# A decode attention kernel: the value stream two tiles behind the key stream, the last values in finer pieces, loops on DVE and ACT as on TensorE

## The chip, the cores and the metric

The kernel runs on one core of a Trainium2 chip. The metric is the device time of one execution in microseconds (us); lower is better. The kernel before took 664.19 us (median of 3 runs, 663.47 to 664.40). The profile gives a span, from the first to the last instruction, which is about 2 us shorter than the device time. Engines are named as the profile names them: PE is TensorE (PEld its weight loads), DVE the vector engine, ACT the scalar engine, POOL is GpSimd, and SP issues the loads. SBUF is the on-chip memory, PSUM the one that takes TensorE's products. The releaser of a wait is what ended it.

## The reference

One token per sequence (4 sequences) attends to a cache of 8192 positions with 8 key/value heads of width 256; each pair of query heads shares one. The result is projected with `wo` and multiplied by a gate from a small MLP-like block.

```python
def _A_ref(x, k_cache, v_cache, wq, wo):                 # x: 4 x 1 x 448
    q = (x @ wq).reshape(B, 1, 16, 256).transpose(0, 2, 1, 3)
    k = jnp.repeat(k_cache, 2, axis=1)                   # cache: 4 x 8 x 8192 x 256, bf16
    v = jnp.repeat(v_cache, 2, axis=1)
    p = softmax(einsum("bhqd,bhkd->bhqk", q, k) * 256 ** -0.5)
    o = einsum("bhqk,bhkd->bhqd", p, v)
    return o.transpose(0, 2, 1, 3).reshape(B, 1, 4096) @ wo
xn = layernorm(A_x)
out = A_x + _A_ref(xn, ...) * silu(_B_ref(xn, ...))      # B: two layernorms, gelu, small weights
```

What matters: 32 tiles (4 sequences x 8 heads), each with 4 MiB of keys and 4 MiB of values, which are read once. With the weights that is 279 MB.

## The kernel before

Keys and values have two slots each in SBUF. For each tile `h` TensorE transposes the keys in 16 groups (`f_t`), DVE and ACT copy the transposed groups out of PSUM, and TensorE forms the scores (`f_s`). Maximum, exponentials and row sum follow. The products of tile `h - 1` with its values (`f_pv`, 128 of them) are spread through the end of tile `h`. TensorE runs this in a hardware loop over pairs of tiles; DVE, ACT and GpSimd have all 32 tiles written out. SP issues all loads on one queue, so the order of its program is the order of the stream.

```python
    PV_PARTS = (0, 12, 24, 44, 72, 100, NPV)
    NPIECE = 4
    ...
            def load_k(h):
                if h >= 2:
                    sp.wait_ge(S["p_t"], NGR * (h - 1))          # keys of h-2 transposed
                sp.dma_start(kn_dst(h), A_k_cache[b, g]...)
            def load_v(h):
                if h == 0:  sp.wait_ge(S["p_h2"], 1)
                else:       sp.wait_ge(S["p_pv"], h)             # products of h-2 done
                ...                                              # the last one in 4 equal pieces
            load_k(0); load_k(1); <wo>; load_v(0)
            for h in range(2, NH):
                load_k(h)
                load_v(h - 1)
            load_v(NH - 1)
    ...
            def body(h):                                         # TensorE, inside its loop
                for j in range(NGR):
                    f_t(h, j)
                    if j >= LAG: f_s(h, j - LAG)
                tail = [three last f_s] + [f_rmaxT(h), f_bc(h), f_sum(h)]
                for i, f in enumerate(tail):
                    f_pv(h - 1, PV_PARTS[i], PV_PARTS[i + 1])
                    f()
    ...
            for h in range(NH):                                  # DVE, written out 32 times
                for j in D_GROUPS: evac(v, h, j)
                f_rmax(h); f_diag(h); f_negb(h); f_ot(h - 1); f_rz(h)
    ...
            take("v_ot")                                         # TensorE, behind its loop
            for g in range(HKV - 1): f_o(g)                      # 7 of 8 output groups, 16 products each
            for i in range(NPIECE):  <last value products, 32 for each piece>
            take("v_ot"); f_o(HKV - 1)
```

## Time and profile before

| | kernel before |
|---|---|
| device time | 664.19 us |
| span of the profiled run | 661.7 us |
| bytes read | 278.99 MB, 98.4% of the DMA engines' span |
| TensorE / DVE / ACT busy | 82% / 39% / 39% |
| last keys landed / last value byte landed | 635.47 / 655.04 us |
| last value product ended | 658.16 us |

The head of the page of the kernel before, with the DMA lines: share of the span per engine, then per fortieth of the span the busy tenths and the GB/s, then the queues (packets, MB, share of 16 engines).

```profile
span 661.7 us, 27809 instructions
PE 543.4 (82%) x12935; PEld 535.1 (81%) x12935; DVE 256.4 (39%) x577; ACT 255.3 (39%) x358; POOL 9.3 (1%) x44
DMA  8999999999999999999999999999999999999993
GB/s 362 436 408 432 422 434 432 428 436 432 430 434 428 436 430 428 438 430 430 436 426 434 434 424 440 428 432 434 428 432 436 424 438 432 430 434 430 428 420 156
...
q1 hardware_dynamic: 12288, 278.99, 98.4%
q8 instruction: 11, 0.18, 0.1%
q14 instruction: 8, 0.07, 0.0%
...
```

The stream is full from the second fortieth to the last but one, so this kernel lives at the speed of its DMA. Queues q8 and q14 carry the engines' own programs.

The next lines are from the timeline of the kernel before, for its end (start, duration, engine, line, operation, count, and in brackets the idle time before and what ended it).

```profile
635.57 3.35 PE L469 MATMUL pst<-ident_b,kn 128*128 128x128 bf16 x32 [2.16 <-PEq L421]
...
652.08 2.72 PE L537 MATMUL pst<-wo_sb,OT 128*4 128x112 bf16 x112 [0.18 <-PEq L421]
654.73 0.61 PE L550 MATMUL psv<-pT,vb 128*128 128x32 bf16 x16
...
657.61 0.55 PE L550 MATMUL psc<-pT,vb 128*128 128x32 bf16 x16
658.21 0.17 DVE L396 TENSOR_TENSOR OT<-psv,rz 128x2 bf16<-128x2 f32 x1 [6.10 <-PE psc L550]
...
658.58 0.37 PE L537 MATMUL pst<-wo_sb,OT 128*4 128x112 bf16 x16 [0.42 <-PEq L421]
...
659.62 0.69 SPq L159 DMA_DIRECT2D out_dram<-out_b  x2
```

The last keys land at 635.47 and TensorE begins at 635.57. From there it has no idle time worth naming until the last value product ends at 657.61 + 0.55 = 658.16: 22.7 us of work from the last key. The finish is 3.54 us. The last value byte had landed 3.1 us before that product ended, so at this end TensorE is late, not the stream.

The trace also records each landing on the semaphores, 16 counts for each load. The Trainium skill (DMA: Bandwidth & Descriptors, section "Why a DMA increments its semaphore by 16 and not by 1") says why: a load runs on up to 16 engines that finish independently, and each posts its own count. The trace agrees: the counts of a load are spread. First and last landing of some loads, in us (load 6 is `wo`; from there on keys and values alternate, in another order after the change):

```
load number        6       10      21      41      61      67 (V30)   71 (last piece)
before, first    47.87    86.79  193.61  387.87  582.13   640.41     650.34
before, last     49.73    90.04  196.89  391.19  585.93   645.19     655.04
```

From load 21 to load 67 the first engine takes 9.713 us for each load of 4 MiB. The distance between first and last grows from 1.9 to 4.8 us. The load is done only with the last one. "First engine" and "last engine" below mean the first and the last landing of a load, as the records name no engine.

### The profile page before, as it was taken

How to read it: one execution, taken by the hardware profiler on the slowest of the kernel's cores; microseconds unless marked ns; L12 is line 12 of the kernel's file. 1: busy time of each engine (PE TensorE's matmuls, PEld its weight loads, DVE VectorE, ACT ScalarE, POOL GpSimd, SP SyncE). 2: the span in 40 equal slices, each digit the busy share in tenths (PEclk: the TensorE clock that was granted, in tenths of full speed). 3: DMA queues.
4: the chain of work that ended last, by engine and by line, in shares of the span. 5: the costliest groups of instructions: out<-in, count | busy, mean ns of one | idle time of the engine just before them, and what ended most of it. 6: DMA issues, size and time to landing. Idle time of an engine off the chain costs nothing. (4 is left out here: it accounts for less than half of the span.)

```text
span 661.7 us, 27809 instructions
## 1 busy us (share of the span) xinstructions
PE 543.4 (82%) x12935; PEld 535.1 (81%) x12935; DVE 256.4 (39%) x577; ACT 255.3 (39%) x358; POOL 9.3 (1%) x44
## 2 busy tenths in 40 slices
PE   2387798889878878988888898878898888789787
PEld 2387797789878878988788898878898788789787
DVE  6233253334433334433334443333344333344332
ACT  1044253344443334444333444433344433344441
POOL 2000000000000000000000000000000000000000
PEclk9988698898877889878789987878988778898788
DMA  8999999999999999999999999999999999999993
GB/s 362 436 408 432 422 434 432 428 436 432 430 434 428 436 430 428 438 430 430 436 426 434 434 424 440 428 432 434 428 432 436 424 438 432 430 434 430 428 420 156
DMA packets 12331, 279.24 MB, mean 422 GB/s; under 512 B 1172, under 2 KB 3224, under 8 KB 3480
## 3 DMA queue, kind: packets, MB, share of 16 engines
q1 hardware_dynamic: 12288, 278.99, 98.4%
q8 instruction: 11, 0.18, 0.1%
q14 instruction: 8, 0.07, 0.0%
q10 hardware_dynamic: 24, 0.01, 0.0%
HBM read 278.99 MB, written 0.00 MB: 422 GB/s over the span
## 5 line engine op out<-in xcount | busy, mean ns | idle before, releaser
L469 PE MATMUL pst<-ident_b,kn 128*128 128x128 bf16 x4096 | 354.4, 244 | 80.7 <-PEq L421 80.7
L469 PEld LDWEIGHTS pst<-ident_b,kn 128*128 128x128 bf16 x4096 | 287.9, 111 | 82.5 <-issue 82.5
L239 ACT ACTIVATE kT<-pst 128x1024 bf16<-128x1024 bf16 x224 | 229.3, 1024 | 231.9 <-PE pst L469 231.9
L237 DVE COPY kT<-pst 128x1024 bf16<-128x1024 bf16 x288 | 197.8, 692 | 268.3 <-PE pst L469 268.3
L481 PE MATMUL psc<-qc,kT 128*128 128x2 bf16 x4096 | 176.8, 164 | 1.0 <-issue 1.0
L481 PEld LDWEIGHTS psc<-qc,kT 128*128 128x128 bf16 x4096 | 157.4, 98 | 1.1 <-issue 1.1
L507 PE MATMUL psv<-pT,vb 128*128 128x32 bf16 x4096 | 131.8, 177 | 5.7 <-issue 3.1
L507 PEld LDWEIGHTS psv<-pT,vb 128*128 128x128 bf16 x4096 | 117.8, 97 | 6.8 <-issue 5.9
L260 ACT ACTIVATE pT<-psc,negb 128x64 bf16<-128x64 f32 x64 | 20.2, 332 | 144.5 <-DVE negb L384 144.5
L372 DVE TENSOR_REDUCE rmax<-psc 128x2 f32<-128x128 f32 x32 | 9.3, 292 | 42.1 <-PE psc L481 42.1
L396 DVE TENSOR_TENSOR OT<-psv,rz 128x2 bf16<-128x2 f32 x65 | 7.6, 162 | 30.1 <-PE psv L507 24.0
L498 PE MATMUL psm<-rowsum,ones_f 128*128 128x2 f32 x64 | 11.8, 253 | 8.5 <-PEq L421 8.5
L498 PEld LDWEIGHTS psm<-rowsum,ones_f 128*128 128x128 f32 x64 | 9.9, 195 | 10.8 <-issue 10.8
L377 DVE TENSOR_REDUCE gmax<-psm 2x1 f32<-2x128 f32 x32 | 8.9, 279 | 17.6 <-PE psm L489 17.6
L493 PE MATMUL psm<-diag,ones_f 2*128 2x2 f32 x64 | 11.6, 248 | 4.5 <-PEq L421 3.9
L493 PEld LDWEIGHTS psm<-diag,ones_f 2*128 2x128 f32 x64 | 9.8, 190 | 6.8 <-issue 4.0
L230 POOL COPY qc<-qT 128x4 bf16<-128x4 bf16 x32 | 6.0, 188 | 599.9 <-PE psc L481 587.1
L384 DVE COPY negb<-psm 128x2 f32<-128x2 f32 x32 | 5.1, 160 | 21.4 <-PE psm L493 21.4
L260 ACT ACTIVATION_READ_ACCUMULATOR pT<-psc,negb 128x1 f32 x64 | 12.6, 196 | 0.0
L427 PE MATMUL pst<-ident_b,xn_b 4*128 4x4 bf16 x14 | 0.6, 161 | 12.6 <-DVE xn_b L306 8.0
L427 PEld LDWEIGHTS pst<-ident_b,xn_b 4*128 4x128 bf16 x14 | 0.5, 99 | 12.7 <-issue 7.9
L388 DVE RECIPROCAL rz<-psm 128x2 f32<-128x2 f32 x32 | 5.5, 171 | 12.6 <-PE psm L498 12.6
(68 smaller groups left out, 70.7 us busy)
## 6 DMA issues: line engine op xcount, KB each, us to landing
kn<-in_A_k_cache_dram SPq DMA_DIRECT2D x32, 4096.0 KB, 27.2
vb<-in_A_v_cache_dram SPq DMA_DIRECT2D x31, 4096.0 KB, 32.3
vb<-in_A_v_cache_dram SPq DMA_DIRECT2D x4, 1024.0 KB, 17.9
vb<-in_A_wq_dram SPq DMA_DIRECT2D x1, 3584.0 KB, 11.5
wo_sb<-in_A_wo_dram SPq DMA_DIRECT2D x1, 3584.0 KB, 46.4
vb<-in_B_w_dram SPq DMA_DIRECT2D x2, 1568.0 KB, 16.9
out_dram<-out_b SPq DMA_DIRECT2D x2, 0.9 KB
out_dram<-out_b ACTq DMA_DIRECT2D x2, 0.9 KB
```

Source lines behind the costliest of these rows:

```text
L230: gp.tensor_copy(qc[:, h % 2], qT[:, b, g]).then_inc(S["g_q"], 1)
L237: engine.tensor_copy(dst, src).then_inc(S["v_ev"], 1)
L239: engine.activation(dst, src, ACT.Copy).then_inc(S["a_ev"], 1)
L260: ins = act.activation(pv_p[:, :, hh], sc[:, :, hh], ACT.Exp, bias=negb[:, s, hh:hh + 1], scale=SCALE, accum_out=rowsum[:, s, hh:hh + 1])
L372: v.tensor_reduce(rmax[:, :], psc[h % 2][:, 0:NCH * REP].rearrange("p (k h) -> p h k", h=REP), AX.X, ALU.max).then_inc(S["v_rmax"], 1)
L377: c(v.tensor_reduce(gmax[:, :], psm[0:REP, 0:P], AX.X, ALU.max))
L396: ins = v.tensor_tensor(OT[:, g, :, dh, b], src[:, dh * PVW:dh * PVW + REP], rz[:, h % 2, :], ALU.mult)
L469: ins = pe.transpose(dst[:, t * P:(t + 1) * P], kn[:, h % 2, GC * j + kl, half * P:(half + 1) * P], ident_b[:, :])
L481: ins = pe.matmul(psc[h % 2][:, kk * REP:(kk + 1) * REP], kT[:, j % RING, t * P:(t + 1) * P], qc[:, h % 2, half, :], start=(half == 0), st ...
L493: pe.matmul(psm[:, P:P + REP], ones_f[0:REP, :], diag[:, :], start=True, stop=True).then_inc(S["p_m2"], 1)
L498: pe.matmul(psm[:, P + REP:P + 2 * REP], ones_f[:, :], rowsum[:, h % 2, :], start=True, stop=True).then_inc(S["p_m3"], 1)
L507: ins = pe.matmul(psv[:, dh * PVW:(dh + 1) * PVW], vb[:, h % 2, kk, dh:DH:NHALF], pT[:, h % 2, kk * REP:kk * REP + PVW], start=(kk == 0), ...
```

## The change

The intent: let the stream end with three value tiles instead of two after the last keys, so that all key work is done while values still arrive; cut the last value tile into pieces of 32, 16, 8 and 8 chunks (a value tile is 64 chunks of 128 positions), so that little is left after the last byte; and make DVE and ACT run loops, as TensorE does. In these loops every pass repeats the same addresses and counts. So DVE writes to a small `otmp`, from where GpSimd, still written out, copies to `OT`, and each wait for a growing count becomes a wait-and-decrement instruction (`take`). The row sum moves to the start of the next tile. The core of the diff (cuts marked by `...`, and lines left out between hunks):

```diff
-    PV_PARTS = (0, 12, 24, 44, 72, 100, NPV)
+    PV_PARTS = (0, 12, 24, 44, 86, NPV)
+    J_SUM = 3
+    PIECES = (0, 32, 48, 56, NCH)
@@ SP
-                    sp.wait_ge(S["p_t"], NGR * (h - 1))
+                    sp.wait_ge(S["v_k"], h - 1)
@@
+                    sp.wait_ge(S["v_v"], h + 1)
+                    ...                                    # last values:
+                    sp.wait_ge(S["v_k"], h)
+                            kn[:, 1 - h % 2, lo:hi, :]     # into the free key slot
-            load_v(0)
             for h in range(2, NH):
                 load_k(h)
-                load_v(h - 1)
+                load_v(h - 2)
+            load_v(NH - 2)
             load_v(NH - 1)
@@ ACT (DVE likewise)
-            for h in range(NH):
-                for j in range(NGR):
-                    if j not in D_GROUPS: evac(act, h, j)
-                exps(h)
+            with nc.Fori(0, NH // 2, engines=[mybir.EngineType.Activation]):
+                for h in range(2):
+                    ...
@@ TensorE
+                    if j == J_SUM:
+                        f_sum(h - 1)
-                tail += [lambda: f_rmaxT(h), lambda: f_bc(h), lambda: f_sum(h)]
+                tail += [lambda: f_rmaxT(h), lambda: f_bc(h)]
-                    f_pv(h - 1, PV_PARTS[i], PV_PARTS[i + 1])
+                    f_pv(h - 2, PV_PARTS[i], PV_PARTS[i + 1])
@@ TensorE, behind its loop
-            for g in range(HKV - 1):
-                f_o(g)
+            f_sum(h)
+            pe.wait_ge(S["g_f"], 1)
+            for g in range(HKV - 2):
+                f_o(g)
+            f_pv(h - 1, 0, NPV)
+            take(pe, "v_ot")
+            f_o(HKV - 2)
```

More of the change, by code (lines that the diff above doesn't have):

```diff
@@ L77, in bass_recurrent_scan__gqa_block_cached__mixer_s_mlp__decode_kernel @@
     NPV = NCH * NHALF
-    PV_PARTS = (0, 12, 24, 44, 72, 100, NPV)
+    PV_PARTS = (0, 12, 24, 44, 86, NPV)
+    J_SUM = 3
     PVW = 32
-    NPIECE = 4
+    PIECES = (0, 32, 48, 56, NCH)
+    NPIECE = len(PIECES) - 1
     x2d = A_x.rearrange("b s d -> b (s d)")
@@ L97, in bass_recurrent_scan__gqa_block_cached__mixer_s_mlp__decode_kernel @@
         qc = sb("qc", [P, 2, NHALF, REP], BF16)
+        otmp = sb("otmp", [P, 2, NHALF, REP], BF16)
         OT = sb("OT", [P, HKV, REP, NHALF, Bn], BF16)
@@ L135, in bass_recurrent_scan__gqa_block_cached__mixer_s_mlp__decode_kernel @@
             + ["dvl%d" % i for i in range(NPIECE)]
-            + ["p_t", "p_sc", "p_m1", "p_m2", "p_m3", "p_pv", "p_x", "p_q", "p_h", "p_h2", "p_o"]
+            + ["p_td", "p_ta", "p_sc", "p_m1", "p_m2", "p_m3", "p_pv", "p_x", "p_q", "p_h", "p_h2", "p_o"]
             + ["v_ev", "a_ev", "v_rmax", "v_diag", "v_neg", "v_ot", "a_exp", "g_q", "g_c",
-               "v_xT", "v_qT", "v_hT", "v_bout", "v_c", "v_w", "a_c", "v_out"])}
+               "v_s", "v_k", "v_v", "g_o", "g_p", "g_f", "v_xT", "v_qT", "v_hT", "v_bout", "v_c", "v_w", "a_c", "v_out"])}
         vflat = [vb[:, i].rearrange("p c d -> p (c d)") for i in range(2)]
@@ L181, in load_v @@
                 b, g = divmod(h, HKV)
-                if h == 0:
-                    sp.wait_ge(S["p_h2"], 1)
-                else:
-                    sp.wait_ge(S["p_pv"], h)
                 src = A_v_cache[b, g].rearrange("(p c) d -> p c d", p=P)
                 if h < NH - 1:
+                    sp.wait_ge(S["v_v"], h + 1)
                     sp.dma_start(vflat[h % 2], src.rearrange("p c d -> p (c d)")
@@ L190, in load_v @@
                 else:
-                    w = NCH // NPIECE
+                    sp.wait_ge(S["v_k"], h)
                     for i in range(NPIECE):
+                        lo, hi = PIECES[i], PIECES[i + 1]
                         sp.dma_start(
-                            vb[:, h % 2, i * w:(i + 1) * w, :].rearrange("p c d -> p (c d)"),
-                            src[:, i * w:(i + 1) * w, :].rearrange("p c d -> p (c d)")
+                            kn[:, 1 - h % 2, lo:hi, :].rearrange("p c d -> p (c d)"),
+                            src[:, lo:hi, :].rearrange("p c d -> p (c d)")
                         ).then_inc(S["dvl%d" % i], 16)
@@ L211, in prog_sp, with take, put @@
             sp.wait_ge(S["dout"], 16 * NQD)
+        def take(eng, name, n=1):
+            eng.wait_ge(S[name], n).then_inc(S[name], -n)
         def prog_pool(gp):
+            def put(h):
+                b, g = divmod(h, HKV)
+                gp.tensor_copy(OT[:, g, :, :, b],
+                               otmp[:, h % 2].rearrange("p dh r -> p r dh")
+                               ).then_inc(S["g_p"], 1)
+                gp.wait_ge(S["g_p"], h + 1)
+                gp.sem_inc(S["g_o"], 1)
             c = _Chain(gp, S["g_c"])
@@ L219, in prog_pool @@
             c(gp.memset(vflat[1][:, DK * HDH:NCH * DH], 0.0))
+            c(gp.memset(vflat[0][:, DK * FH + NF * D:NCH * DH], 0.0))
+            c(gp.memset(rowsum[:, :, :].rearrange("p s r -> p (s r)"), 1.0))
             c(gp.memset(rz[:, :, :].rearrange("p s r -> p (s r)"), 1.0))
@@ L228, in prog_pool @@
                 if h >= 2:
-                    gp.wait_ge(S["p_sc"], h - 1)
+                    gp.wait_ge(S["v_v"], h - 1)
                 gp.tensor_copy(qc[:, h % 2], qT[:, b, g]).then_inc(S["g_q"], 1)
+                if h >= 4:
+                    put(h - 4)
+            for h in range(NH, NH + 2):
+                gp.wait_ge(S["v_v"], h - 1)
+                put(h - 4)
+            gp.wait_ge(S["g_p"], NH - 2)
+            gp.sem_inc(S["g_f"], 1)
         def evac(engine, h, j):
-            engine.wait_ge(S["p_t"], NGR * h + j + 1)
+            take(engine, "p_td" if j in D_GROUPS else "p_ta")
             src = pst[j % NST][:].bitcast(BF16)
@@ L253, in exps @@
                 s = h % 2
-                act.wait_ge(S["v_neg"], h + 1)
-                if h >= 1:
-                    act.wait_ge(S["p_pv"], h)
+                take(act, "v_neg")
                 sc = psc[s][:, 0:NCH * REP].rearrange("p (k h) -> p k h", h=REP)
@@ L264, in exps @@
                         ins.then_inc(S["a_exp"], 1)
-            for h in range(NH):
-                for j in range(NGR):
-                    if j not in D_GROUPS:
-                        evac(act, h, j)
-                exps(h)
+            with nc.Fori(0, NH // 2, engines=[mybir.EngineType.Activation]):
+                for h in range(2):
+                    for j in range(NGR):
+                        if j not in D_GROUPS:
+                            evac(act, h, j)
+                    exps(h)
             act.wait_ge(S["v_out"], 1)
@@ L310, in prog_dve @@
             v.sem_inc(S["v_ot"], 1)
+            v.sem_inc(S["g_o"], 4)
+            v.sem_inc(S["a_exp"], 1)
+            v.sem_inc(S["dv0"], 16)
             v.sem_inc(S["dv1"], 16)
@@ L321, in prog_dve @@
             xn2_mark = c.n
-            v.wait_ge(S["g_c"], 8)
+            v.wait_ge(S["g_c"], 10)
             idv = ident_f[:, :].rearrange("p (m t) -> p t m", t=NHF)
@@ L370, in f_rmax @@
             def f_rmax(h):
-                v.wait_ge(S["p_sc"], h + 1)
+                take(v, "p_sc")
                 v.tensor_reduce(rmax[:, :], psc[h % 2][:, 0:NCH * REP].rearrange(
@@ L375, in f_diag @@
             def f_diag(h):
-                v.wait_ge(S["p_m1"], h + 1)
-                c(v.tensor_reduce(gmax[:, :], psm[0:REP, 0:P], AX.X, ALU.max))
-                c.sync()
+                take(v, "p_m1")
+                v.tensor_reduce(gmax[:, :], psm[0:REP, 0:P], AX.X, ALU.max
+                                ).then_inc(S["v_s"], 1)
+                take(v, "v_s")
                 v.tensor_scalar(diag[:, :], ident_f[0:REP, 0:REP], gmax[:, 0:1], -SCALE,
@@ L382, in f_negb @@
             def f_negb(h):
-                v.wait_ge(S["p_m2"], h + 1)
+                take(v, "p_m2")
                 v.tensor_copy(negb[:, h % 2, :], psm[:, P:P + REP]).then_inc(S["v_neg"], 1)
             def f_rz(h):
-                v.wait_ge(S["p_m3"], h + 1)
-                c(v.reciprocal(rz[:, h % 2, :], psm[:, P + REP:P + 2 * REP]))
+                take(v, "p_m3")
+                v.reciprocal(rz[:, h % 2, :], psm[:, P + REP:P + 2 * REP]
+                             ).then_inc(S["v_s"], 1)
@@ L390, in f_ot @@
+                take(v, "v_s")
             def f_ot(h):
-                b, g = divmod(h % NH, HKV)
-                v.wait_ge(S["p_pv"], h + 2)
-                c.sync()
+                take(v, "p_pv")
+                take(v, "g_o")
+                v.tensor_tensor(otmp[:, h % 2],
+                                psv[:, 0:NHALF * PVW].rearrange("p (a n) -> p a n", a=NHALF)[
+                                    :, :, 0:REP],
+                                rz[:, h % 2, :].unsqueeze(1).broadcast_to([P, NHALF, REP]),
+                                ALU.mult).then_inc(S["v_s"], 1)
@@ new lines, in f_ot @@
+                take(v, "v_s")
+                v.sem_inc(S["v_ot"], 1)
+                v.sem_inc(S["v_v"], 1)
+            with nc.Fori(0, NH // 2, engines=[mybir.EngineType.DVE]):
+                for h in range(2):
+                    for j in range(NGR):
+                        if j in D_GROUPS:
+                            evac(v, h, j)
+                        if j == J_SUM + 1:
+                            f_rz(h - 1)
+                    v.sem_inc(S["v_k"], 1)
+                    f_rmax(h)
+                    f_diag(h)
+                    f_ot(h - 2)
+                    f_negb(h)
@@ L394, in f_ot @@
+            f_rz(NH - 1)
+            for h in (NH - 2, NH - 1):
+                b, g = divmod(h, HKV)
+                take(v, "p_pv")
                 for dh in range(NHALF):
                     src = psc[0] if (h == NH - 1 and dh == 1) else psv
-                    ins = v.tensor_tensor(OT[:, g, :, dh, b], src[:, dh * PVW:dh * PVW + REP],
+                    ins = v.tensor_tensor(OT[:, g, :, dh, b],
+                                          src[:, dh * PVW:dh * PVW + REP],
                                           rz[:, h % 2, :], ALU.mult)
-                    if dh == NHALF - 1:
-                        ins.then_inc(S["v_ot"], 1)
-                    else:
-                        c(ins)
@@ L403, in prog_dve @@
-            for h in range(NH):
-                for j in range(NGR):
-                    if j in D_GROUPS:
-                        evac(v, h, j)
-                f_rmax(h)
-                f_diag(h)
-                f_negb(h)
-                f_ot(h - 1)
-                f_rz(h)
-            f_ot(NH - 1)
+                ins.then_inc(S["v_ot"], 1)
             v.wait_ge(S["p_o"], 1)
@@ L419, in prog_pe @@
         def prog_pe(pe, xn_mark, xn2_mark):
-            def take(name, n=1):
-                pe.wait_ge(S[name], n).then_inc(S[name], -n)
-            pe.wait_ge(S["g_c"], 8)
+            pe.wait_ge(S["g_c"], 10)
             for k, (src, mark) in enumerate(((xn_b, xn_mark), (xn2_b, xn2_mark))):
@@ L431, in prog_pe @@
                 if k == 0:
-                    take("v_xT")
-            take("dwq", 16)
+                    take(pe, "v_xT")
+            take(pe, "dwq", 16)
             qo = q_ps[:, 0:NKC * Bn].rearrange("p (b a g dh hh) -> p g hh dh a b", b=Bn, a=NHF,
@@ L442, in prog_pe @@
             ins.then_inc(S["p_q"], 1)
-            take("dw3", 16)
-            take("v_xT")
+            take(pe, "dw3", 16)
+            take(pe, "v_xT")
             w3v = w3_sb.rearrange("p j (m k) -> p j k m", k=NFK)
@@ L450, in prog_pe @@
             ins.then_inc(S["p_h"], 1)
-            take("dw4", 16)
-            take("v_hT")
+            take(pe, "dw4", 16)
+            take(pe, "v_hT")
             for k in range(NFK):
@@ L460, in prog_pe @@
             ins.then_inc(S["p_h2"], 1)
-            take("v_bout")
+            take(pe, "v_bout")
             def f_t(h, j):
                 if j == 0:
-                    take("dk%d" % (h % 2), 16)
+                    take(pe, "dk%d" % (h % 2), 16)
                 dst = pst[j % NST][:].bitcast(BF16)
@@ L471, in f_t @@
                                        ident_b[:, :])
-                ins.then_inc(S["p_t"], 1)
+                ins.then_inc(S["p_td" if j in D_GROUPS else "p_ta"], 1)
             def f_s(h, j):
                 if j == 0:
-                    take("g_q")
-                take("v_ev" if j in D_GROUPS else "a_ev")
+                    take(pe, "g_q")
+                take(pe, "v_ev" if j in D_GROUPS else "a_ev")
                 for t in range(TB):
@@ L487, in f_rmaxT @@
             def f_rmaxT(h):
-                take("v_rmax")
+                take(pe, "v_rmax")
                 pe.transpose(psm[0:REP, 0:P], rmax[:, :], ident_f[:, :]).then_inc(S["p_m1"], 1)
             def f_bc(h):
-                take("v_diag")
+                take(pe, "v_diag")
                 pe.matmul(psm[:, P:P + REP], ones_f[0:REP, :], diag[:, :], start=True, stop=True
@@ L496, in f_sum @@
             def f_sum(h):
-                take("a_exp")
+                take(pe, "a_exp")
                 pe.matmul(psm[:, P + REP:P + 2 * REP], ones_f[:, :], rowsum[:, h % 2, :],
@@ L502, in f_pv @@
                 if lo == 0:
-                    take("v_ot")
-                    take("dv%d" % (h % 2), 16)
+                    take(pe, "v_ot")
+                    take(pe, "dv%d" % (h % 2), 16)
                 for i in range(lo, hi):
@@ L529, in prog_pe @@
             h = NH - 1
-            take("dwo", 16)
+            take(pe, "dwo", 16)
             def f_o(g):
@@ L540, in f_o @@
                 return ins
-            take("v_ot")
-            for g in range(HKV - 1):
+            f_sum(h)
+            pe.wait_ge(S["g_f"], 1)
+            for g in range(HKV - 2):
                 f_o(g)
-            w = NCH // NPIECE
+            f_pv(h - 1, 0, NPV)
+            take(pe, "v_ot")
+            f_o(HKV - 2)
             for i in range(NPIECE):
-                take("dvl%d" % i, 16)
+                take(pe, "dvl%d" % i, 16)
                 for dh in range(NHALF):
-                    for kk in range(i * w, (i + 1) * w):
+                    for kk in range(PIECES[i], PIECES[i + 1]):
                         ins = pe.matmul((psv, psc[0])[dh][:, dh * PVW:(dh + 1) * PVW],
-                                        vb[:, h % 2, kk, dh:DH:NHALF],
+                                        kn[:, 1 - h % 2, kk, dh:DH:NHALF],
                                         pT[:, h % 2, kk * REP:kk * REP + PVW], start=(kk == 0),
@@ L554, in prog_pe @@
             ins.then_inc(S["p_pv"], 1)
-            take("v_ot")
+            take(pe, "v_ot")
             f_o(HKV - 1).then_inc(S["p_o"], 1)
```

## The prediction

> **What bounds the kernel now.** The DMA stream. The page counts 278.99 MB at a mean 422 GB/s, the queue holding 98.4% of 16 engines; the view of equal windows gives 430 to 432 GB/s in every stretch from 60 to 630 us. The landing records show each 4096 KB tile taking 9.71 us per DMA engine without a gap. TensorE is busy 82%, and between tiles it waits for the next keys (29 waits, 80.7 us in the groups view), so it has 2 to 3 us to spare per 19.4 us pair. DVE and ACT are busy 39%.
>
> **Where time can be won: only at the end.** In the timeline the last keys land at 635.5 us, TensorE then works without a pause: keys until 651.5, 112 output products (2.7 us), the last values' 128 products from 654.73 to 658.16, and 3.54 us of finish. The last value bytes land at 655.04, so the chain from the last key, not the last byte, decides the end, by about 3 us.
>
> **What the change does.**
> 1. Values two tiles behind: the stream ends K31, V29, V30, V31 instead of K31, V30, V31. The last keys land about 9.7 us earlier (near 625.7), so key work, the first outputs and all but 16 of the last value products can run under the stream. After the last byte remain about 0.1 us of wait, 16 products (0.5 us) and the same finish, 3.5 us: 655.04 + 4.1 = 659.2 instead of 661.7. At best -2.5 us.
> 2. Pieces of 32, 16, 8, 8 chunks shrink the last piece's products from 32 to 16, about 0.4 us, contained above.
> 3. Loops on DVE and ACT: no busy time removed. Their instruction fetches fall (DVE and ACT now make about six 8192-byte fetches while the stream runs; after, one or two, plus GpSimd's). Engine skew in the landings grows from 3.3 us at tile 4 to 4.8 us at the end, by +0.43 and +0.98 us just after such fetches; without them the last byte comes up to 1.4 us earlier.
> 4. GpSimd copies, one otmp product for two, the later row sums: off the critical path.
>
> **What is lost.** At the start V0 now follows K2. From the present tile times, K4 is issued near 87.5 us while the fastest DMA engine runs dry at 86.8 and the slowest at 90.0: a gap of 1 to 3 us on fast engines, about none on the slow one that decides. In the end phase TensorE's program behind the loop grows from 256 to about 386 products. In the first loop pass each 16384-byte fetch block [...]stalled TensorE 1.0 to 4.0 us (waits with releaser "issue"). The Trainium skill (Runtime: NRT & Kernel Launch, Instruction fetch mechanics) says that fetch is sequential, in 16 KiB blocks; the trace agrees for TensorE. I expect one such stall of 1 to 4 us near the end of the V30 products (648 to 653 us), partly hidden by the stream; it eats about 0.8 us.
>
> **Sum.** -2.5 - 0.7 (skew) + 0.8 (fetch) + 0.5 (start, small pieces) = -1.9 us. Predicted 662.3 us, range 660.0 to 665.0. Faster by over 2%: 0.01; within 2%: 0.97; slower: 0.02.
>
> **Right if:** middle windows stay near 432 GB/s; last keys land near 625; TensorE idles in the last 10 us waiting for value pieces; the last byte lands at 653.5 to 655.5; about 4 us follow it.
>
> **Wrong if:** a short loop crosses a fetch block on ACT (the same section says that a taken branch outside the window forces a fetch), which would show as 8 KB fetches every 39 us and more skew; the gap near 87 us is longer than estimated; the fetch stall in the end phase exceeds 4 us.

## More of the kernel before

The granted clock is the share of full speed at which TensorE's clock ran.

(Landing times in this document are counted from a zero 0.03 to 0.04 us before that of the timeline, in every run; no reading hangs on it.)

## The result, and the profile after

The changed kernel took 662.59 us (median of 4 runs, 661.94 to 663.36) against 663.85 us for the kernel before on the same chip. The ratio is 0.9981 with a 95% interval of 0.9964 to 0.9998. Ratios here are the mean time of one kernel's fast runs over that of the other's in the same rounds, so they are not quite the ratio of the medians. The class is "same" (within 2%), but the gain is clear of noise. A repeat with five rounds gave 0.9975 (0.9962 to 0.9987).

The same lines of the page, for the changed kernel:

```profile
span 660.5 us, 29043 instructions
PE 535.4 (81%) x13065; PEld 530.5 (80%) x13065; DVE 252.3 (38%) x548; ACT 254.9 (39%) x358; POOL 17.0 (3%) x76
DMA  8999999999999999999999999999999999999995
GB/s 363 440 402 434 415 419 427 439 417 433 425 443 429 429 437 423 443 429 429 437 423 441 429 431 435 425 441 429 431 435 425 441 429 431 435 425 441 429 424 208
...
q1 hardware_dynamic: 12288, 278.99, 98.8%
q8 instruction: 11, 0.18, 0.1%
q14 instruction: 2, 0.02, 0.0%
...
```

The fetches on q14 fall from 8 to 2. In the fifth and sixth slices (66 to 99 us) the GB/s row shows 415 and 419, against 422 and 434 before: something is lost at the start. The end of the changed kernel, from its timeline:

```profile
643.82 2.32 PE L574 MATMUL pst<-wo_sb,OT 128*4 128x112 bf16 x96
...
646.08 3.31 PE L542 MATMUL psv<-pT,vb 128*128 128x32 bf16 x122
651.01 0.35 PE L542 MATMUL psv<-pT,vb 128*128 128x32 bf16 x6 [1.61 <-issue]
...
654.94 0.37 PE L590 MATMUL psv<-pT,kn 128*128 128x32 bf16 x8
655.83 0.40 PE L590 MATMUL psc<-pT,kn 128*128 128x32 bf16 x8 [0.52 <-issue]
...
656.28 0.37 PE L590 MATMUL psc<-pT,kn 128*128 128x32 bf16 x8
656.81 0.17 DVE L447 TENSOR_TENSOR OT<-psv,rz 128x2 bf16<-128x2 f32 x1 [5.07 <-DVEq L216]
...
657.19 0.54 PE L574 MATMUL pst<-wo_sb,OT 128*4 128x112 bf16 x16 [0.53 <-PEq L216]
...
658.39 0.67 SPq L162 DMA_DIRECT2D out_dram<-out_b  x2
```

TensorE stops for 1.61 us after 122 of the 128 products of tile 30. The values are there (they landed at 644.57) and the wait has the releaser "issue", that is, nothing that the profile shows. A 16,384-byte fetch of TensorE's program began at 648.70 and took 1.07 us; TensorE went on at 651.01. A second, short stop of the same kind sits in the middle of the third piece, after a second fetch. In the six traces that have the first stop (these are the two-tile runs but x_pool_fetch and x_wide_out) TensorE goes on 1.3 to 1.6 us after the end of that fetch, and in the four that have the second one 1.3 to 1.5 us after the end of the next. The last value product ends at 656.28 + 0.37 = 656.65.

The landings, in us:

```
load number        6       10      21      41      61      67 (V30)   71 (last piece)
after, first     47.78    87.44  195.57  389.86  584.12   642.39     652.30
after, last      50.16    90.47  197.76  392.01  586.28   644.57     655.03
```

The last byte lands at the same time as before (655.03 against 655.04), yet the path to it is quite different. Take the last engine. From load 6 to 21 it needed 147.16 us before and 147.60 us after, and it was already 0.43 us behind at load 6: it is 0.87 us later at load 21. From 21 to 67 the pure stream would need 46 x 9.713 = 446.80 us; it needed 448.30 before and 446.81 after: 1.49 us gained. From 67 to 71 it needed 9.85 before and 10.46 after: 0.61 us lost, at the time of the fetch at 648.70. The sum is 0.87 - 1.49 + 0.61 = -0.01.

The first engine shows what happened at the start. Between loads 6 and 21 it lost 0.04 us before and 2.09 us after against 15 x 9.713 us. The issue times of the queue say why for most of it. SP's own lines of the timeline, before and then after:

```profile
74.67 0.33 SPq L188 DMA_DIRECT2D vb<-in_A_v_cache_dram  x1
86.73 0.33 SPq L177 DMA_DIRECT2D kn<-in_A_k_cache_dram  x1
```

```profile
74.91 0.33 SPq L188 DMA_DIRECT2D vb<-in_A_v_cache_dram  x1
86.09 0.33 SPq L180 DMA_DIRECT2D kn<-in_A_k_cache_dram  x1
```

Before, the load issued at 86.73 is K4, and one more value tile (V2, issued at 74.67) still stood ahead of it in the queue. After, the load issued at 74.91 is only V1, and the first engine had finished it by 87.44; K4, issued at 86.09, came too late to follow without a gap.

Load by load the first engine lost 0.56 us at K3, 0.25 at V1 and 0.63 at K4, which were issued 1.3 to 2.5 us before it ran dry. Another 0.6 us went at loads 15 to 18, all issued over 12 us ahead, so not for late issue; the record does not show the cause, and the repeat has no such loss. For the last engine this matters: from load 6 to load 14 it lost 1.46 us after and 1.47 us before, so with the gap it lost no more than the kernel before without one. (The one-tile runs with loops, which have no gap either, lost 0.4 to 1.0 us there, so the gap may still have cost it up to 1 us.) Its 0.87 us are 0.43 that it was behind at load 6 and 0.44 at loads 15 to 18. A longer gap does reach it: in c_after it lost 3.7 us there.

### The profile page after: what moved, and what is told of

Read it like the earlier page. It is cut to its first block, busy times and chain, and to the rows that moved or that the text cites. A ratio compares the mean times of both kernels' runs of the same rounds, so it can differ in the third digit from the quotient of the medians.

```text
span 660.5 us, 29043 instructions
## 1 busy us (share of the span) xinstructions
PE 535.4 (81%) x13065; PEld 530.5 (80%) x13065; DVE 252.3 (38%) x548; ACT 254.9 (39%) x358; POOL 17.0 (3%) x76
## 5 line engine op out<-in xcount | busy, mean ns | idle before, releaser
L504 PE MATMUL pst<-ident_b,kn 128*128 128x128 bf16 x4096 | 347.0, 241 | 92.7 <-PEq L216 92.6
L542 PE MATMUL psv<-pT,vb 128*128 128x32 bf16 x4224 | 130.3, 177 | 7.8 <-issue 7.7
L542 PEld LDWEIGHTS psv<-pT,vb 128*128 128x128 bf16 x4224 | 119.2, 97 | 8.8 <-issue 8.2
L533 PE MATMUL psm<-rowsum,ones_f 128*128 128x2 f32 x66 | 15.5, 304 | 1.7 <-PEq L216 1.7
L533 PEld LDWEIGHTS psm<-rowsum,ones_f 128*128 128x128 f32 x66 | 13.4, 253 | 1.7 <-issue 1.7
L420 DVE TENSOR_TENSOR otmp<-psv,rz 128x4 bf16<-128x4 f32 x32 | 5.2, 163 | 22.9 <-DVEq L216 22.9
L524 PE MATMUL psm<-ident_f,rmax 128*2 128x128 f32 x32 | 8.8, 276 | 0.0
## 6 DMA issues: line engine op xcount, KB each, us to landing
vb<-in_A_wq_dram SPq DMA_DIRECT2D x1, 3584.0 KB, 11.2
```

Source lines behind the costliest of these rows:

```text
L504: ins = pe.transpose(dst[:, t * P:(t + 1) * P], kn[:, h % 2, GC * j + kl, half * P:(half + 1) * P], ident_b[:, :])
L524: pe.transpose(psm[0:REP, 0:P], rmax[:, :], ident_f[:, :]).then_inc(S["p_m1"], 1)
L533: pe.matmul(psm[:, P + REP:P + 2 * REP], ones_f[:, :], rowsum[:, h % 2, :], start=True, stop=True).then_inc(S["p_m3"], 1)
L542: ins = pe.matmul(psv[:, dh * PVW:(dh + 1) * PVW], vb[:, h % 2, kk, dh:DH:NHALF], pT[:, h % 2, kk * REP:kk * REP + PVW], start=(kk == 0), ...
```

## The experiments

All twelve gave correct results, and all were timed or looked at beside the kernel before. "Start" is the time that the first engine lost between loads 6 and 21, "middle" the time that the last engine lost between loads 21 and 67, both against 9.713 us per load. Last byte, last product and the two losses are of the profiled run; the span is the median of the runs (for the kernel before, of all its runs in these rounds).

| run | ratio (95%) | span | start | middle | last byte | last product ended |
|---|---|---|---|---|---|---|
| before | | 661.6 | 0.0 | 1.50 | 655.04 | 658.16 |
| c_before | | 660.7 | 0.0 | 1.50 | 655.16 | 657.18 |
| changed | 0.9981 (0.9964-0.9998) | 660.5 | 2.1 | 0.01 | 655.03 | 656.65 |
| c_after, repeat | 0.9975 (0.9962-0.9987) | 660.25 | 3.6 | 0.12 | 658.03 | 658.80 |
| x_unrolled | 1.0070 (1.0055-1.0085) | 666.7 | 0.0 | 5.54 | 659.82 | 660.47 |
| x_lag_only | 0.9997 (0.9983-1.0010) | 661.9 | 4.2 | 3.95 | 661.75 | 662.39 |
| x_loops_only | 0.9997 (0.9983-1.0010) | 661.7 | 0.0 | 0.08 | 653.63 | 657.29 |
| c_loops_only | | 661.1 | 0.0 | 0.04 | 653.53 | 657.46 |
| x_lag1_loops | 1.0005 (0.9992-1.0017) | 662.1 | 0.0 | 0.07 | 653.46 | 658.31 |
| x_lag1_fill | 0.9977 (0.9964-0.9991) | 659.7 | 0.0 | 0.07 | 653.42 | 656.03 |
| x_reorder | 0.9975 (0.9960-0.9991) | 660.05 | 2.0 | 0.08 | 654.15 | 655.58 |
| x_pieces16 | 1.0016 (0.9998-1.0035) | 661.7 | 1.9 | 0.01 | 654.86 | 656.03 |
| x_pool_fetch | 1.0163 (1.0148-1.0179) | 672.65 | 3.7 | 11.28 | 668.35 | 669.00 |
| x_wide_out | 1.0059 (1.0044-1.0075) | 665.35 | 3.6 | 0.01 | 655.09 | 659.18 |

Theory A, formed after the first result: the loops help because they remove instruction fetches, each of which delays one DMA engine; the two-tile lag wins at the end about what it loses at the start. Theory B: the lag brings the gain, the loops are neutral.

### c_after: the changed kernel again

No edit.

> The changed kernel again, as a control beside the other three. Expected ratio to the kernel before 0.997 to 0.999, span near 660.5 us, last value byte near 655.0 us, TensorE stalled about 1.7 us six products before the end of the V30 products and about 0.6 us inside the last-but-one piece, two 8192-byte fetches during the stream.

Measured: ratio 0.9975, as expected. The profiled run was the odd one of six, at 662.4 us, while the other five had spans of 660.2 to 660.3. It shows how the start varies: K4 was issued at 87.90 instead of 86.09, the first engine lost 3.64 us instead of 2.09, and the last byte came at 658.03. The expected place of the last byte was missed for that reason. The stop after 122 products was there again (2.05 us), and the second one was 0.29 us.

### x_unrolled: the changed kernel with the two loops written out

```diff
-            with nc.Fori(0, NH // 2, engines=[mybir.EngineType.Activation]):
+            for _ in range(NH // 2):
-            with nc.Fori(0, NH // 2, engines=[mybir.EngineType.DVE]):
+            for _ in range(NH // 2):
```

> Changed kernel with the DVE and ACT loops unrolled, all else kept. Theory A (the loops help, because fewer instruction fetches steal time from single DMA engines; the start of the two-tile lag costs as much as it wins): 8 to 14 fetches of 8192 bytes during the stream, engine skew of the landings before the last values 3 to 4.5 us instead of 2.2, last byte 656 to 657.5 us, span 661.5 to 663, so about as slow as the kernel before. Theory B (the value lag alone brings the gain at the end, loops are neutral): span 660 to 661 as the control.

Measured: 1.0070, slower by more than expected. The fetches of 8,192 bytes between 80 and 650 us rose to 15, the last engine fell back step by step until it was 8.6 us behind the first at load 67, and the last byte came at 659.82 although the first engine had no start loss at all (K4 was issued at 84.4 here). The wait-and-decrement instructions make the written-out programs longer than those of the kernel before, hence more fetches than there.

### x_lag_only: the lag without the loops

The same, with the waits of DVE, ACT and GpSimd counted up, so that no decrement is needed:

```diff
         def take(eng, name, n=1):
-            eng.wait_ge(S[name], n).then_inc(S[name], -n)
+            if eng is nc.tensor or getattr(eng, "engine", None) == mybir.EngineType.PE:
+                eng.wait_ge(S[name], n).then_inc(S[name], -n)
+            else:
+                seen[name] = seen.get(name, 0) + n
+                eng.wait_ge(S[name], seen[name])
```

> The changed kernel with DVE and ACT unrolled and their waits counted up as before the change, so that no wait-and-decrement instructions lengthen their programs; two-tile lag, pieces and later row sum kept. Theory A: 7 to 10 fetches of 8192 bytes during the stream, skew 3.5 to 4.8 us, last byte 656 to 657, span 661 to 662.5, ratio to before 0.998 to 1.001: the lag alone wins little. Theory B: 660 to 660.7, ratio 0.997.

Measured: 0.9997, as theory A expected, with spans from 660.9 to 665.9. The profiled run was the slowest; there both losses are large, 4.2 us at the start and 3.95 us in the middle, and the last byte at 661.75 was far past the expected 656 to 657. Lag, finer pieces and later row sum without the loops give nothing on average.

### x_loops_only and c_loops_only: the loops without the lag

From the changed kernel, lag, order of the loads, pieces and row sum put back (shortened):

```diff
-                load_v(h - 2)
+                load_v(h - 1)                # and load_v(0) ahead of the loop, as before
-                    f_pv(h - 2, ...)
+                    f_pv(h - 1, ...)
-                    if j == J_SUM: f_sum(h - 1)
+                tail += [..., lambda: f_sum(h)]
-    PIECES = (0, 32, 48, 56, NCH)
+    PIECES = (0, 16, 32, 48, NCH)            # and into the value slot
```

> The kernel before with only the loops on DVE and ACT (and the GpSimd copy that a loop needs): value stream one tile behind, row sum at the end of the same tile, pieces of 16 chunks, all as before. Theory A (fewer instruction fetches on one DMA engine is a gain of its own; the earlier one-tile run lost it only because its late row sum left TensorE idle 1.7 us in the end chain): skew about 3.3 us instead of 4.8, last keys near 634.0, chain of 22.7 us from there as before, last product near 656.7, span 660 to 660.7, ratio to before about 0.9975. Theory B (loops are neutral, the lag brings the gain): span 661.5 to 662.2, ratio 0.999 to 1.001.

> A second look at the kernel before with loops only, whose timed runs (median span 661.7 us) were slower than its profiled run (660.9). Expected: middle loss of the slowest DMA engine 0.0 to 0.2 us again, last keys 634 to 635; where the span is 661.7, either the last keys come later through the start, or the chain after them is longer than 23.3 us.

Measured: 0.9997. The half of theory A about the stream held in both looks: the middle loss fell from 1.50 to 0.08 and 0.04 us, the last keys landed at 634.00 and 633.90 instead of 635.47, the last byte at 653.63 and 653.53. The other half did not: the work from the last key to the last value product took 23.3 and 23.6 us instead of 22.7, and 21.7 in the second look at the kernel before. The output groups began 17.2 and 17.8 us after the last key, against 16.6 and 16.8. In those chains the waits that the loops need stand before the small products: in the first look TensorE waits 0.25 us ahead of the broadcast, where it did not wait before, 0.47 instead of 0.28 us ahead of the row sum, and 0.29 instead of 0.18 us ahead of the output groups, now for the GpSimd copy; that is 0.55 us together (the lines below). The second look also came to its first value products 0.6 us later after its key. The rest differs with the granted clock at that place, which was 0.66 and 0.72 from 650 to 655 us in the two looks at the loops and 0.72 and 1.00 in the two at the kernel before. So most of the 1.5 us that the stream wins is spent again on a chain that the stream does not bound: 0.55 us of it on waits, the rest not separated from the clock. Both looks were quicker (660.9 and 661.1) than the median run (661.7), which has no trace. The lines of the kernel before, and then of x_loops_only:

```profile
650.11 0.35 PE L493 MATMUL psm<-diag,ones_f 2*128 2x2 f32 x2
651.54 0.35 PE L498 MATMUL psm<-rowsum,ones_f 128*128 128x2 f32 x2 [0.28 <-PEq L421]
```

```profile
648.90 0.35 PE L524 MATMUL psm<-diag,ones_f 2*128 2x2 f32 x2 [0.25 <-PEq L216]
650.53 0.35 PE L529 MATMUL psm<-rowsum,ones_f 128*128 128x2 f32 x2 [0.47 <-PEq L216]
651.17 2.78 PE L568 MATMUL pst<-wo_sb,OT 128*4 128x112 bf16 x112 [0.29 <-POOLq L252]
```

### c_before: a second look at the kernel before

No edit.

> A second look at the kernel before: is the 4.8 us skew of its trace typical? Expected 3.8 to 5.5 us before the last values, seven 8192-byte fetches during the stream, last keys 634.5 to 636, span 661 to 662.

Measured: the trace is typical. The middle loss is 1.50 us again, the distance at load 67 is 4.8 us, the last keys land at 635.53. It ended 1 us earlier than the first look because the 112 output products took 1.5 instead of 2.7 us at the higher clock.

### x_lag1_loops and x_lag1_fill: one tile of lag, later row sum

The first is the changed kernel with one tile of lag; the second adds the fill: five of the seven first output groups go ahead of the last row sum.

```diff
-                load_v(h - 2)
+                load_v(h - 1)
-                    f_pv(h - 2, ...)
+                    f_pv(h - 1, ...)         # last values in their own slot; this is x_lag1_loops
@@ x_lag1_fill only
+            pe.wait_ge(S["g_p"], NH - 3)
+            for g in range(HKV - 3): f_o(g)
             f_sum(h)
             pe.wait_ge(S["g_f"], 1)
-            for g in range(HKV - 1): f_o(g)
+            for g in range(HKV - 3, HKV - 1): f_o(g)
```

> Changed kernel with the value stream one tile behind the keys as before, last values into their own value slot; loops, pieces of 32,16,8,8 and the later row sums kept. Theory A: no dry DMA engines at the start, skew near 2.5 to 3.3 us, last keys land near 634 us instead of 635.5, TensorE's chain from there is as long as before (22.7 us), so last product near 656.7 and span 660 to 661: as fast as the changed kernel. Theory B: without the lag the gain is lost, span 661.5 to 662, ratio to the kernel before 1.000.

> The one-tile run with loops and late row sum again, now with five of the seven output groups (80 products) ahead of the last row sum, so that the 1.7 us of TensorE idleness there is filled. If that idleness is what cost the one-tile version its gain: last product 1.7 us earlier against the last keys, near 656.6 us with a last byte near 653.5, span 660.3, ratio to before 0.997 to 0.998, equal to the changed kernel; the two-tile lag would then be worth nothing over this. If the lag itself is needed: span 661.5 to 662, ratio 0.999 to 1.001.

Measured: 1.0005 for the first, so theory A missed it, and 0.9977 for the second. The lines of the two ends, first without and then with the fill:

```profile
651.75 0.56 PE L533 MATMUL psm<-rowsum,ones_f 128*128 128x2 f32 x2 [1.68 <-PEq L217]
652.24 2.77 PE L574 MATMUL pst<-wo_sb,OT 128*4 128x112 bf16 x112
...
657.96 0.35 PE L588 MATMUL psc<-pT,vb 128*128 128x32 bf16 x8
```

```profile
651.87 0.35 PE L533 MATMUL psm<-rowsum,ones_f 128*128 128x2 f32 x2 [0.56 <-PEq L217]
652.16 0.57 PE L574 MATMUL pst<-wo_sb,OT 128*4 128x112 bf16 x32
...
655.68 0.35 PE L591 MATMUL psc<-pT,vb 128*128 128x32 bf16 x8
```

Without the fill TensorE waits 1.68 us for the last row sum, because the later row sum leaves nothing between the last products and the exponentials; with five output groups moved there it waits 0.56. The last product comes 2.3 us earlier; part of that is the clock, which was 0.66 in the first and 1.00 in the second from 650 to 655 us. The one-tile order with loops and the fill is as fast as the changed kernel. The two-tile lag is therefore one way of keeping TensorE's chain out of the end, and not the only one. It also avoids the loss at the start, which is 0.0 us in all one-tile runs. The fill without the loops was not run, so how much of the 0.9977 is due to the loops is not separated.

### x_reorder: the same fill in the changed kernel

```diff
+            pe.wait_ge(S["g_p"], NH - 3)
+            for g in range(HKV - 3): f_o(g)
             f_sum(h)
             pe.wait_ge(S["g_f"], 1)
-            for g in range(HKV - 2): f_o(g)
+            f_o(HKV - 3)
             f_pv(h - 1, 0, NPV)
```

> Changed kernel with five of the six first output groups (80 products) moved ahead of the last row sum, where TensorE idles 1.7 us; it then enters the next block of its program earlier. If the instruction fetch bounds the end phase: the stall before the last six V30 products falls from 1.7 to under 1 us, the one in the pieces vanishes, the last product ends 0.6 us after the last byte (655.6 instead of 656.65), span about 659.5, 1.0 us less than the control. If the landing of the value bytes bounds it: no change, 660.5.

Measured: 0.9975, equal to the repeat of the changed kernel. The place of the stop in the timeline:

```profile
644.04 3.31 PE L542 MATMUL psv<-pT,vb 128*128 128x32 bf16 x122 [0.90 <-PEq L216]
650.21 0.34 PE L542 MATMUL psv<-pT,vb 128*128 128x32 bf16 x6 [2.86 <-issue]
```

TensorE reached the end of its block 2 us earlier than in the changed kernel, but the next block came only 0.8 us earlier (the fetch began at 647.7 instead of 648.7), so the stop grew to 2.86 us. The second one shrank to 0.25 us, and the last product ended 1.43 us after the last byte, not the 0.6 us hoped for. The profiled run's 1.1 us over the changed one is mostly its earlier last byte. That the stop belongs to the fetch is supported by its place, the same product in all two-tile runs with these output products except x_pool_fetch, and by the 1.3 to 1.6 us from the fetch's end to TensorE's next product. In those six runs the fetch began 1.5 to 3.7 us after this block of products did; in x_pool_fetch it began after 0.5 us (660.43 against 659.92), early enough for no stop. That the stop costs the time after the last byte was not shown by taking it away.

### x_pieces16: the last values in four equal pieces

```diff
-    PIECES = (0, 32, 48, 56, NCH)
+    PIECES = (0, 16, 32, 48, NCH)
```

> Changed kernel with the last values in four pieces of 16 chunks. If the last byte bounds the end: 32 instead of 16 products after it, 0.4 us more, last product about 1.0 to 1.2 us after the last byte landed; if the program fetch of TensorE bounds it (it ended 1.6 us after the last byte in the changed kernel): within 0.3 us of the changed kernel. Ratio to before 0.997 to 0.999 either way.

Measured: 1.0016 (0.9998 to 1.0035), outside the expected ratio, but not by the pieces alone as far as the trace tells. The profiled run has a span of 659.8 us, and its last product ended 1.17 us after the last byte, as expected for the case that the last byte bounds the end, with TensorE waiting 1.22 us for the last piece. In that run the coarse pieces lost nothing against the changed kernel's 1.62 us. The three timed runs had spans of 660.8 to 662.9, and their device times exceed the spans by 2.5 to 3.2 us, more than usual. The worth of the finer pieces stays open; nothing here shows one.

### x_pool_fetch: more program on an idle engine

```diff
                 if h >= 4:
                     put(h - 4)
+                for _ in range(48):
+                    gp.sem_inc(S["g_x"], 1)
+                    gp.wait_ge(S["g_x"], 1).then_inc(S["g_x"], -1)
```

> Changed kernel plus 96 idle semaphore instructions per tile on GpSimd, which has nothing else to do: about 24 more instruction fetches of 8192 bytes, no more work on any engine that matters. Theory A (fetches steal time from one DMA engine, 0.5 to 1.0 us each, and the slowest engine decides): skew grows step by step, by 10 to 20 us if the fetches of GpSimd fall on one engine, 2 to 4 if they are spread; span grows by 2 to 18 us. Rival (the unrolled kernel was slow for another reason, such as slower DVE and ACT sequencing): no change, span 660 to 662.5, skew 2.2 to 2.6.

Measured: 1.0163, 10.8 us slower than the kernel before (means). GpSimd still waited 530 us for DVE, no engine is seen to wait for its copies in the loop, and no other engine got more instructions. The queue lines of its page:

```profile
q1 hardware_dynamic: 12288, 278.99, 97.2%
q14 instruction: 26, 0.21, 0.1%
```

There were 26 fetches against 2 in the changed kernel, together 0.21 MB of 279. The last engine was 11.2 us behind the first at load 67 and had lost 11.28 us in the middle, while 17 fetches fell into that stretch. That is 0.7 us for each, though a fetch itself took 0.32 us. For the same stretch the other runs show 5 fetches and 1.50 us (before), 7 and 3.95 (x_lag_only), 11 and 5.54 (x_unrolled), 1 and at most 0.12 (the runs with loops). Theory A is confirmed for this step, and the rival, that DVE and ACT are merely slower to sequence when written out, is not needed: the dose works on an engine that no other is seen to wait for.

The traces settle more than these sums. Add up the 16 landings of each load from 21 to 67: every one of the 40 fetches in x_pool_fetch, x_unrolled, x_lag_only and the kernel before cost 0.5 to 1.1 us in that sum, in the load in which it fell or in the next, and all other loads lost at most 0.1 us, but for load 67 of x_pool_fetch, which was issued after the first engine had run dry. In x_pool_fetch the last engine alone lost as much as the sum, about 0.65 us at each of 17 steps, and at load 67 fifteen engines landed from 647.4 to 648.3 us and one at 658.5. So there a fetch put one engine back and left the other 15 alone. Where the engine hit was not the last one, nothing was lost at the end: of the kernel before's five fetches only those at 459 and 596 us moved the last landing, by 0.43 and 0.98 us.

### x_wide_out: fewer products behind the loop

```diff
-    NQD = 4
+    NQD = 1                                  # one product of 448 columns instead of four of 112
+            for _ in range(42):                  # ahead of TensorE's loop
+                pe.transpose(pst[0][:].bitcast(BF16)[:, 0:P], ident_b[:, :], ident_b[:, :])
```

> Changed kernel with the output projection as one product of 448 columns in place of four of 112 (28 products fewer by 84 in the end phase), 42 idle transposes added ahead of the loop so that the loop keeps its place against the fetch blocks. If the fetch of TensorE's program in the end phase costs the time between last byte and last product: one 16384-byte fetch before the end instead of two, no stall in the V30 products, last product 0.5 to 0.7 us after the last byte instead of 1.4 to 1.6. The finish itself grows by about 0.7 us, since DVE works on 448 columns instead of 112, so the total stays within 0.5 us of the changed kernel: 0.9970 to 0.9985. If the fetch costs nothing: last product still 1.4 us or more after the last byte.

Measured: 1.0059; the experiment failed in its purpose. The stop within the tile 30 products did vanish (all 128 stand in one row of the timeline), but the first 24 wide products took 7.4 us where 96 narrow ones took 2.3, so TensorE was late for another reason and its last product ended 4.1 us after the last byte. Part of that is the granted clock, 0.50 for the first 15 of them (0.37 us each) and 1.00 for the rest (0.19 us), against 0.54 for the narrow ones. The four narrow products of a quartet, 0.10 us together, write different partitions, and the times suggest that they overlap; no run tested that. What the fetch costs at the end was therefore not measured by itself.

## Why the prediction was right

The predicted 662.3 us stands against 662.59, well inside 660.0 to 665.0. Point by point:

1. *Only the end can be won.* Right. The stretch from 200 to 400 us moved 432 GB/s in both kernels.
2. *Last keys about 9.7 us earlier, near 625.7.* Right: 625.15, and TensorE's key work was done by 641.
3. *Fewer fetches bring the last byte up to 1.4 us earlier.* The mechanism was right, as the middle loss (1.50 to 0.01 us) and the dose on GpSimd show. Its size was put at 0.7 us in the sum and was 1.49.
4. *The gap at the start costs the slowest engine about none.* Right for the gap in this run, measured against the kernel before: the first engine lost 1.4 us in it, inside the 1 to 3 predicted, and the last one lost no more than before. But the last engine was 0.87 us later at load 21 for two other reasons, 0.43 us that was there at load 6 already and 0.44 us at loads 15 to 18, where the cause is open. Over the runs the start is the unsteady part: 1.9 to 4.2 us in the two-tile runs, except 0.0 where K4 was issued at 84.4 us; in c_after, where the first engine lost 3.6 us, the last one lost 3.7.
5. *One fetch stop of 1 to 4 us near the end of the V30 products.* Right in place and size: 1.6 us, six products before their end, going on at 651.0. The short stop in the third piece was not predicted, nor that the last DMA engine would lose 0.61 us while the fetch ran. "TensorE idles for value pieces" was wrong: it idled for its own program and for DVE's hand-over.
6. *About 4.1 us after the last byte.* Wrong as a term: it was 660.5 - 655.03 = 5.5, where 4.1 and 0.8 for the fetch had been allowed. The last product ended 1.62 us after the byte instead of 0.6, and the finish took 3.83 us instead of 3.54; TensorE's granted clock there was lower (the window lines below), the 16 last output products took 0.54 us instead of 0.37, and TensorE waited 0.53 us ahead of them instead of 0.42.

The window lines from 655 to 662 us, of the kernel before and of the changed one: the busy time and count of PE, PEld, DVE, ACT and POOL, with the granted clock, the DMA share and the GB/s in the last three columns:

```profile
655.00:662.00 7.00, 3.54 (x141) 3.29 (x137) 0.78 (x4) 0.00 (x0) 0.00 (x0) 0.96 0.01 3
```

```profile
655.00:662.00 7.00, 1.68 (x52) 1.24 (x48) 0.79 (x4) 0.00 (x0) 0.00 (x0) 0.50 0.01 2
```

So the total came out inside the range with terms off in opposite directions, and that it lies within 0.3 us of the forecast is luck. The loops won 1.49 us of stream where 0.7 was assumed; 0.87 us by load 21 and 0.61 us at the time of TensorE's fetch took it back, where 0.5 was allowed for the start; the end after the last byte was 0.6 us longer than allowed. The gain was 1.3 us (663.85 to 662.59) where 1.9 was predicted. The prediction treated the two parts of the change as a sum. The runs show that they are not: loops alone 0.9997, lag alone 0.9997, both 0.9975 to 0.9981 (the intervals of loops alone and of both still touch; the median spans are 661.7 and 660.25 to 660.5 us). The loops win 1.5 us of stream, which counts only if TensorE's chain is not what ends last; the lag takes that chain away, but without the loops it ends on a late stream. None of the versions tried clearly beats the changed kernel; two equal it (x_reorder, and x_lag1_fill with the one-tile lag).

What stays open: the cost of TensorE's fetch at the end taken by itself, the worth of the small pieces, the loss at loads 15 to 18 of the changed kernel, and which DMA engine serves which fetch, as the records name no engine.

## What to carry to other kernels

When a stream fills all DMA engines, look at the last engine's landing and not at the mean: a fetch of an engine's program that is nothing in bytes can put one DMA engine back, and a load waits for that one. Short loops on helper engines can be worth more to the stream than to the engines, but only if the work after the last byte bounds the end; check which chain ends last before adding up gains. A longer distance between two streams also means fewer tiles in flight until the first slot comes free, so look for the price at the start of what is won at the end.

## What the Trainium skill lacked or had wrong

- *Runtime: NRT & Kernel Launch*, section "Instruction fetch mechanics", gives refills in blocks of 16 KiB. TensorE's fetches were 16,384 bytes here, but those on q14, which fell when DVE and ACT got loops and rose when GpSimd's program grew, were 8,192 bytes.
- The same section calls the cost of crossing a block "mostly hidden". Under a full stream it was not: TensorE stopped 1.0 to 3.9 us four times in its first pass of the kernel before (1.04 and 3.15 us with the releaser "issue", 2.55 and 3.89 us with TensorE's own sequencer, PEq; each time it went on 1.4 to 1.8 us after the end of a fetch), and 1.6 to 2.9 us in the end of the two-tile kernels with loops (not in the one with wide output products, nor in x_pool_fetch, where the fetch began early).
- The same section warns that a taken branch outside the window forces a fetch. The loops on DVE and ACT showed the other side: 16 passes each, and one fetch between 80 and 640 us.
- No page says what a fetch costs a DMA engine that is streaming. *DMA: Bandwidth & Descriptors*, section "Queues, rings and completion order", says that an engine takes turns between queue rows at packet boundaries. A fetch took 0.32 us, and each of 40 fetches cost the 16 landings of a load 0.5 to 1.1 us in their sum, which is one engine put back by that much; the run with 24 more of them took 12 us longer.
- No page gives a figure for the spread between the 16 engines over a long stream: 1.1 to 4.8 us at load 67 in the kernels with few fetches, 7 to 11 us in those with many.
